# A convolution by two-step Fourier transforms on one Trainium2 core: real and imaginary rows contracted in one matmul, two column halves side by side

## The chip, the cores and the metric

The kernel runs on one core of one Trainium2 chip (trn2). The metric is the device time of one execution in microseconds, lower is better. A kernel is executed several times; the times and their median are given, and one further execution carries the hardware profiler. Engines are named as in the profile: PE is TensorE (PEld its weight loads), DVE VectorE, ACT ScalarE, POOL GpSimd, SP SyncE.

## The reference

Two branches read the same `x` (2048 rows, 640 columns, bfloat16); a gate per row mixes them.

```python
def reference(A_x, A_wqkv, A_wo, B_u, B_A_re, ..., B_Dskip, gate_w):
    # branch A: 32 heads of 20; each position attends to itself and 7 earlier
    # ones, 2 apart
    qkv = x @ wqkv
    logits = einsum("bhsd,bhswd->bhsw", q, kg) * scale     # 8 positions each
    o = einsum("bhsw,bhswd->bhsd", softmax(logits), vg)
    a = o @ wo
    # branch B: per column d a filter K of 2048 taps, then a long convolution
    P = exp(dt * A[:, :, None] * arange(L))                # D x 192 x L
    K = einsum("dn,dnl,dn->dl", C, P, dt * B).real
    y = irfft(rfft(pad(u)) * rfft(pad(K)))[:L] + u * Dskip
    g = sigmoid((x * gate_w).sum(-1, keepdims=True))
    return g * a + (1 - g) * y                              # u is x
```

## The kernel before

The program has two parts, each a list of tasks whose order over all engines is a table of numbers (`ORDER["main"]`, `ORDER["tail"]`): a row says which task comes next and, with a letter, on which engine an eviction runs (A for ACT, D for DVE). `Plan.emit` writes the instructions in that order, and each engine keeps its own part of it, first in, first out. `Plan.add` gives each task a duration, its dependencies (`deps`), order-only predecessors (`after`) and the buffers that it takes and gives back; the durations serve the search that made the table and reach no instruction.

"main" (to about 245 us) does the attention, the gate and the filter taps, and the first step of both Fourier transforms. `KGen` makes the taps: argument matmuls (L827), sines and exponentials on ACT (L842, L844), products on DVE (L864, L866), and small matmuls in four column groups of 32 (L882, into `kps`). The attention of 256 rows at a time is: products on DVE (L384), logits (L390), weighted values on DVE (`pv`, L453), their sums over heads in two column halves (L460, the "gathers"), and the output projection (L484) with its eviction (L493 or L495).

A transform of 4,096 points is split into 32 times 64. The **first step** is the 32-point one. Its data lie with partitions (4 column groups g, 32 times t1). One unit of it, made by `first` or `split` in `gated_mix_kernel`, yields 1,024 numbers in each of 128 partitions: the filter's first half of columns in ten units `f1`, its second half in ten units `fk` (five of them cut in two by `split`, which uses the `tb` buffers of the attention), the input's in twenty units `fu`. The data are the weights of the matmul, taken as every `st`-th column of `kc` (the filter) or `Usb` (the input), and a table of cosines and sines is streamed:

- `f1`, `fk` (L1329, halves L1352): four matmuls a unit, each with 128 columns of weights that lie 40 elements (80 bytes) apart and 256 streamed columns.
- `fu` (L1325): eight matmuls a unit, in two halves of the rows (64 partitions each, side by side), each with 128 columns of weights that lie 80 elements (160 bytes) apart and 128 streamed columns. The table is block diagonal, so each row half needs only its own half of it.

The result stands in a two-bank PSUM tile of the pool `ar`, of which there are two, and ACT or DVE evicts it (`evict`, L511 or L513) into `bufA` (filter, `Bk`) or `big` (input). In both, a partition is (c2, t2): c2 is one of two halves of the columns of x, t2 one of 64 times; and the free index f of 64 is (32 frequencies f1, real or imaginary).

"tail" (`fft_conv`) begins with the **second step**, for eight blocks `fb` of four frequencies f1. A unit (`trans`, L1095) makes the real (ro = 0) or imaginary (ro = 1) spectrum of two frequencies, of filter (k) or input (u): four matmuls of 128 by 128 weights and 320 streamed columns. The weights come from a table `phis` that holds the 64-point matrix twice on the diagonal, once for each c2, in the three forms real, imaginary and minus imaginary; for each frequency, a matmul on the real columns and one on the imaginary ones add up in PSUM. Each unit is evicted on ACT or DVE (`ev`) into `sp_k` or `sp_u`. Six DVE products and sums a block (`ta`, `tc`, L1123; `Y`, L1126) multiply the spectra. Then come the inverse steps (L1156, evictions into `bufA`; L1186) and the mix with the attention's result (L1192, L1195, L1200), and the stores (L1213).

The table `phis` takes eight loads of 4 frequencies: three from POOL in "main" (`load_phi`, tag `PHI`), three on SP at the start of the tail into tiles `PHX` (`more`), two more on SP into freed `PHI` tiles. The units of blocks 3 to 7 depend on their load (`ready`). SP also loads `psi` and the attention's result `gaF`, paced by the evictions (`paced`).

Of the kernel before, what the change touches and what calls it, by code (L numbers as in the profile page):

```python
# [13 lines left out]
F32 = mybir.dt.float32  # L14
# [26 lines left out]
def _attn_consts():  # L41
# [929 lines left out]
def _fft_consts():  # L971
# [6 lines left out]
    for g in range(4):  # L978
        f1b[g, :, g, :] = f1c.reshape(32, 64)
# [23 lines left out]
def fft_prefetch(ctx, tc, x, omS, keep):  # L1003
# [12 lines left out]
    def load_phi(k, eng=nc.gpsimd):  # L1016
        t = pre.tile([128, 4, 3, 128], BF16, name="PHI", tag="PHI", bufs=3)
        eng.dma_start(t[:], phi_d[:, 4 * k:4 * k + 4])
        return t
# [413 lines left out]
```

## Time and profile before

| | before |
|---|---|
| median of 3 runs | 314.68 us (314.07 to 315.07) |
| the profiled execution | 316.68 us |
| its span, first to last instruction | 314.9 us |
| PE, DVE, ACT busy | 286.3, 285.9, 285.2 us |
| mean granted TensorE clock | 0.978 |
| first step, `fu` units | 218.1 to 238.5 us |
| second step, first to last matmul | 244.75 to about 281.9 us |

In the profile's rows, `x` is a count; a row of the timeline gives start, duration (from the first start to the last end of a merged group), engine, line, operation, and out<-in. `128*64` beside a matmul is its weights' rows and columns, `128x320` what it streams. In the windows view each stretch has the busy time and the count of each engine, the granted clock, the share of the DMA engines and GB/s.

### The profile page before, as it was taken

The page shows a single profiled execution, that of the slowest core. Times are in us where ns is not written, and L with a number is a line of the kernel's source. Part 1 is how long each engine was busy: PE and PEld are TensorE (multiplying, and loading weights), DVE is VectorE, ACT ScalarE, POOL GpSimd, SP SyncE. Part 2 cuts the span into 40 slices and gives each one's busy share as a digit, 9 for nine tenths or more (in the row PEclk, how much of TensorE's full clock was granted, in tenths as well). Part 3 has the DMA queues.
Part 4 walks back from the last instruction along what each step waited for, and adds up shares of the span by engine and source line. Part 5 has one row for each costly group of instructions (what it writes and reads, how often), then busy time and mean ns, then how long its engine had stood idle before and what let it go on. Part 6 is the DMA issues. An engine that isn't in the chain of part 4 may idle for free. (4 is left out here: it accounts for less than half of the span.)

```text
span 314.9 us, 12073 instructions
## 1 busy us (share of the span) xinstructions
PE 286.3 (91%) x5268; PEld 169.8 (54%) x5268; DVE 285.9 (91%) x381; ACT 285.2 (91%) x431; POOL 56.9 (18%) x84
## 2 busy tenths in 40 slices
PE   8799999999999999999999989789999999979740
PEld 3455543444554554555555555447668676659730
DVE  4988999999999989999999999999888899998881
ACT  2789869999999999999999999999989799997890
POOL 8722440302000001111302022020120000000072
PEclk9799999999999999999999999999999999997995
DMA  7995679286111304537795694742493366591076
GB/s 260 363 237 140 183 200 168 81 176 149 24 36 21 106 8 122 108 89 214 192 264 126 127 212 94 153 103 79 169 334 115 131 214 167 113 167 20 4 174 161
DMA packets 47182, 45.70 MB, mean 145 GB/s; under 512 B 27034, under 2 KB 40650, under 8 KB 47130
## 3 DMA queue, kind: packets, MB, share of 16 engines
q1 hardware_dynamic: 40776, 26.68, 32.7%
q0 software_dynamic: 5392, 17.53, 21.7%
q8 instruction: 41, 0.67, 0.9%
q10 hardware_dynamic: 962, 0.73, 0.8%
q14 instruction: 11, 0.09, 0.1%
HBM read 29.60 MB, written 14.01 MB: 138 GB/s over the span
## 5 line engine op out<-in xcount | busy, mean ns | idle before, releaser
L319 PE MATMUL tb<-bufA 128*128 128x512 bf16 x300 | 76.4, 390 | 1.6 <-DMA bufA<-in_A_wqkv_dram 1.2
L842 ACT ACTIVATE big<-ar 128x740 bf16<-128x740 int16 (+1 forms) x72 | 57.6, 876 | 0.2
L827 PE MATMUL ar<-Rarg,L 64*128 64x212 bf16 (+4 forms) x600 | 47.8, 251 | 5.0 <-ACT big L842 2.2
L844 ACT ACTIVATE big<-ar 128x848 bf16<-128x848 f32 x60 | 49.8, 903 | 0.5 <-PE ar L827 0.2
L319 PEld LDWEIGHTS <-bufA 128*128 128x128 bf16 x300 | 31.8, 121 | 30.3 <-issue 9.9
L453 DVE TENSOR_TENSOR pv<-vc,asb 128x2048 bf16<-128x2048 bf16 x40 | 47.7, 1217 | 0.2 <-PE tb L460 0.2
L827 PEld LDWEIGHTS <-L 64*128 64x128 bf16 x600 | 20.7, 94 | 33.7 <-issue 30.8
L864 DVE TENSOR_TENSOR pt<-big 128x1024 bf16<-128x1024 bf16 x48 | 32.2, 702 | 1.5 <-PE kps L882 0.8
L882 PEld LDWEIGHTS <-pt 128*32 128x32 bf16 (+1 forms) x2560 | 23.1, 92 | 11.6 <-issue 9.4
L882 PE MATMUL kps<-qq,pt 128*32 128x21 bf16 (+1 forms) x2560 | 28.1, 174 | 0.6 <-ACT E L511 0.3
L484 PE MATMUL tb<-wo_sb,oT 128*128 128x320 bf16 x160 | 27.7, 301 | 0.9 <-ACT ga L493 0.7
L384 DVE TENSOR_TENSOR prod<-qA,kA 128x2048 bf16<-128x2048 bf16 x20 | 23.8, 1219 | 0.4 <-PE lg L390 0.3
L511 ACT ACTIVATE sp_u<-fp 128x640 bf16<-128x640 f32 x30 | 22.4, 876 | 1.7 <-PE fp L1095 1.7
L384 DVE TENSOR_TENSOR prod<-prj 128x2048 bf16<-128x2048 bf16 x20 | 23.8, 1218 | 0.0
L460 PE MATMUL tb<-pv,ind 128*64 128x512 bf16 (+1 forms) x192 | 22.3, 350 | 0.3 <-DVE pv L453 0.3
L511 ACT ACTIVATE sp_k<-fp 128x640 bf16<-128x640 f32 x30 | 22.2, 883 | 0.4 <-PE fp L1095 0.4
L866 DVE TENSOR_TENSOR qq<-big 128x1344 bf16<-128x1344 bf16 x24 | 21.2, 884 | 0.0
L1213 POOL DMA_DIRECT2D out_dram<-ot x14 | 7.8, 560 | 71.3 <-PE yp L1186 68.8
L1095 PEld LDWEIGHTS <-PHI 128*128 128x128 bf16 x160 | 15.6, 98 | 7.8 <-issue 1.8
L377 POOL DMA_DIRECT2D vc<-vS x16 | 11.5, 726 | 44.5 <-DVE pv L453 39.6
L484 PEld LDWEIGHTS <-oT 128*128 128x128 bf16 x160 | 13.5, 97 | 8.1 <-issue 3.6
L493 ACT ACTIVATE ga<-tb,g_sb 128x320 bf16<-128x320 f32 x28 | 15.2, 570 | 0.0
(171 smaller groups left out, 525.6 us busy)
## 6 DMA issues: line engine op xcount, KB each, us to landing
vc<-vS POOLq DMA_DIRECT2D x16, 327.5 KB, 5.4
gaS<-ga SPq DMA_DIRECT2D x8, 320.0 KB
Usb<-in_A_x_dram POOLq DMA_DIRECT2D x8, 320.0 KB, 5.0
gaF<-gaS SPq DMA_DIRECT2D x8, 320.0 KB
bufA<-in_A_wqkv_dram SPq DMA_DIRECT2D x3, 800.0 KB
L<-Sprm SPq DMA_DIRECT2D x76, 30.0 KB
asb<-aS SPq DMA_DIRECT2D x16, 128.0 KB
psi<-c_psi SPq DMA_DIRECT2D x4, 512.0 KB
```

The costliest lines, as they stand in the source:

```text
L319: nc.tensor.matmul(ppf, self.wq[:, which, kt, e::5], self.xT[:, c0 // 1024, kt, c0 % 1024:c0 % 1024 + SC], start=(kt == 0), stop=(kt == NK ...
L384: nc.vector.tensor_tensor(b[e][:], q[:, e, o:o + C].unsqueeze(1).to_broadcast([128, W, C]), win(k[:, e, :], o, W, DIL, C), ALU.mult)
L453: nc.vector.tensor_tensor(o, vw, b["asb"][:].unsqueeze(2).to_broadcast(sh), ALU.mult)
L460: nc.tensor.matmul(b["op", e][64 * a:64 * a + 64, 0:n, :], ind[:, 32:96], b["pv", e][:, w, a, 0:n, :], start=(w == 0), stop=(w == 3), skip ...
L484: nc.tensor.matmul(apf[:, :320], b["oT"][:, e, i * 128:(i + 1) * 128], wo_sb[:, e, hf * 320:(hf + 1) * 320], start=(e == 0), stop=(e == 4))
L511: nc.scalar.activation(o, i, ACT.Identity)
L827: nc.tensor.matmul(ar[:, g2, a0:a0 + ncol], L[rows, sb, gv, l0:l0 + 128], R[rows, c0:c0 + ncol], start=True, stop=True, tile_position=(64 ...
L842: nc.scalar.activation(d_[:, :, s0 * QW:s1 * QW], ar[:].bitcast(I16)[:, :, 0:2 * (s1 - s0) * QW:2], ACT.Sin, scale=SCL)
L844: nc.scalar.activation(dst[:, gp::2].rearrange("p g s n -> p g (s n)"), ar[:, :, 0:2 * EW], ACT.Exp)
L864: nc.vector.tensor_tensor(pt[:, :, k, :], gg[:, :, ::-1] if k else gg, e1, ALU.mult)
L866: nc.vector.tensor_tensor(qq[:], trg[:, :, KI:].rearrange("p a (v m) -> p a v m", v=2), exq[:, :, KI:].unsqueeze(2).to_broadcast([128, 32, ...
L882: nc.tensor.matmul(kps[32 * g:32 * g + 32, h, NM * ql:NM * ql + NM], pt[rows, k, v, :], qq[rows, k, v, :], start=(g not in started), stop= ...
```

## The change

The first step now puts real and imaginary parts into partitions: its tables are laid out as (real or imaginary, f1, g), a matmul takes only 64 columns of weights (t2, for one c2) and streams 128 columns, and the real part goes to PSUM partitions 0 to 63, the imaginary part to 64 to 127 (`tile_position=(0, 64 * r)`). All units, `fu` too, have one form: sixteen matmuls in eight such pairs, both of a pair with the same 64 weight columns. Those lie twice as far apart as before: 80 elements (160 bytes) in `kc`, 160 elements (320 bytes) in `Usb`. The odd and even units are now the two c2, so that the free index f of `bufA` and `big` is (f1, c2).

In the second step, real and imaginary rows are then contracted in one matmul of 128 rows: a unit has four matmuls, two frequencies times two c2; each has 64 columns of weights and 320 streamed columns, and the two c2 go to the two column halves. Nothing accumulates over two matmuls any more. The table has two forms of 64 columns for each frequency and is a third as large. Three loads from POOL, of 12, 12 and 8 frequencies, hold all of it, so the five loads in the tail and their waits are gone.

Both parts of `ORDER` are new numbers. Of the planned durations, `fu` goes from 0.25 to 0.47, `f1` and `fk` from 0.437 to 0.47, a half from 0.22 to 0.24, a unit of the second step from 0.566 to 0.28.

```diff
 ORDER = {"main": (
-    "0 14 40 -53 3 51 -5 -47 -1 49 -45 1D 45 1 9 1 -55 -3 4 13 43 1 -55 45 -46 54 -6 9D 4 1 -15 16 -46D 2 -17 47D 9 1 1 -57 "
...
+    "0 14 -13 3 6 -8 5D 43 1 -48 49 1 -47 2 46 1 7 1 1 1 -56 57 1D 4 1 -14 -2 -45 1 -7 68 -16 20 1 1D 4 1 -25 -37 -9 72D "
...
+    f1b = f1b.reshape(4, 32, 4, 32, 2).transpose(0, 1, 4, 3, 2)
     f1c = f1b.reshape(128, 256)
...
-    phis = np.zeros((64, 2, 32, 3, 2, 64), np.float32)
-    for c2 in range(2):
-        phis[:, c2, :, 0, c2, :] = Phi.real.transpose(1, 0, 2)
-        phis[:, c2, :, 1, c2, :] = Phi.imag.transpose(1, 0, 2)
-        phis[:, c2, :, 2, c2, :] = -Phi.imag.transpose(1, 0, 2)
-    phis = phis.reshape(128, 32, 3, 128)
+    pr, pi = Phi.real.transpose(1, 0, 2), Phi.imag.transpose(1, 0, 2)
+    phis = np.stack([np.stack([pr, pi], axis=2), np.stack([-pi, pr], axis=2)], axis=0).reshape(128, 32, 2, 64)
...
     def load_phi(k, eng=nc.gpsimd):
-        t = pre.tile([128, 4, 3, 128], BF16, name="PHI", tag="PHI", bufs=3)
-        eng.dma_start(t[:], phi_d[:, 4 * k:4 * k + 4])
+        n = min(12, 32 - 12 * k)
+        t = pre.tile([128, 12, 2, 64], BF16, name="PHI", tag="PHI", bufs=3)
+        eng.dma_start(t[:, 0:n], phi_d[:, 12 * k:12 * k + n])
...
-    early = []
-    for k in range(3, 6):
...
-        early.append(pl.add(f"tphi{k}", "S", 0.4, more, after=early[-1:], dma=1.6))
...
-                        for ri in range(2):
-                            kind = (0 if ri == 0 else 2) if ro == 0 else (1 if ri == 0 else 0)
-                            nc.tensor.matmul(fp[:, fl % 2, 0:320].rearrange("p (c x) -> p c x", x=32), phis[fb][:, fl, kind, :],
-                                             B[:, :, 2 * f1 + ri].rearrange("p c q g -> p c (q g)"), start=(ri == 0), stop=(ri == 1))
+                        for c2 in range(2):
+                            nc.tensor.matmul(fp[64 * c2:64 * c2 + 64, fl % 2, 0:320].rearrange("p (c x) -> p c x", x=32), phis[f1 // 12][:, f1 % 12, ro, :],
+                                             B[:, :, 2 * f1 + c2].rearrange("p c q g -> p c (q g)"), start=True, stop=True, skip_group_check=True, tile_position=(0, 64 * c2))
...
-                if name == "fu":
-                    by = b["by"] = b["bp"][:].rearrange("p a (b f) -> p (a b) f", f=64).rearrange("p (g q) f -> p g q f", g=4)
-                    for ql in range(4):
-                        for r in range(2):
-                            nc.tensor.matmul(by[:, 2 * r:2 * r + 2, ql], sf[64 * r:64 * r + 64, 4 * n + ql::st], P["F1c"][64 * r:64 * r + 64, 128 * r:128 * r + 128],
-                                             start=True, stop=True, skip_group_check=True, tile_position=(64 * r, 0))
-                    return
-                for ql in range(4):
-                    nc.tensor.matmul(b["bp"][:, ql, :], sf[:, 4 * n + ql::st], P["F1k"][:], start=True, stop=True)
+                st = sf.shape[1] // 64
+                b["bp"] = pa.tile([128, 8, 128], F32, name="bp", tag="ar")
+                F = P["F1c" if name == "fu" else "F1k"][:].rearrange("p (r x) -> p r x", r=2)
+                for q in range(8):
+                    for r in range(2):
+                        nc.tensor.matmul(b["bp"][64 * r:64 * r + 64, q, :], sf[:, 8 * (n // 2) + q + st // 2 * (n % 2)::st], F[:, r],
+                                         start=True, stop=True, skip_group_check=True, tile_position=(0, 64 * r))
...
+                evict(nc, en, d_[:, n // 2, n % 2::2], b["bp"][:].rearrange("p q (f g) -> p f q g", g=4))
```

What this makes of the order is shown at three places. The first is PE while the last chunk's attention ends, between its gathers (`tb` from `pv`) and the input's units (`bp` from `Usb`). Before, two units of eight matmuls stood together between gathers of eight:

```order
L460 LDWEIGHTS ind_82
L460 MATMUL tb_5694<-pv_102,ind_82 64x512
...
L1325 LDWEIGHTS Usb_3743
L1325 MATMUL bp_5705<-F1c_73,Usb_3743 128x2x64
...
L1325 MATMUL bp_5715<-F1c_73,Usb_3743 128x2x64
...
L460 MATMUL tb_5726<-pv_102,ind_82 64x512
```

In the changed kernel, a unit of sixteen matmuls stands after every four of a gather:

```order
L460 LDWEIGHTS ind_82
L460 MATMUL tb_5834<-pv_102,ind_82 64x512
...
L1308 LDWEIGHTS Usb_3790
L1308 MATMUL bp_5839<-F1c_73,Usb_3790 64x128
...
L460 MATMUL tb_5834<-pv_102,ind_82 64x512
...
L1308 MATMUL bp_5866<-F1c_73,Usb_3790 64x128
...
L460 MATMUL tb_5884<-pv_102,ind_82 64x512
```

A gather is now cut in two by a unit. After the last `kps` matmul of the taps, PE has twenty `fu`, one `f1` and ten `fk` units where it had eighteen, one and ten.

The second place is PE where the first step ends and the second begins (`fp` from `big` or `bufA` and the table `PHI`). Before, the filter's units came last and the input's spectrum first:

```order
L1352 MATMUL tb_5960<-F1k_74,kc_5889 128x256
L1095 LDWEIGHTS PHI_5919
L1095 MATMUL fp_5990<-big_605,PHI_5919 128x320
...
L1095 MATMUL fp_5995<-big_605,PHI_5919 128x320
...
L1095 MATMUL fp_6003<-bufA_78,PHI_5919 128x320
```

Now an input unit comes last and the filter's spectrum first:

```order
L1308 MATMUL bp_6351<-F1c_73,Usb_3790 64x128
L1079 LDWEIGHTS PHI_6055
L1079 MATMUL fp_6390<-bufA_78,PHI_6055 64x320
...
L1079 MATMUL fp_6395<-bufA_78,PHI_6055 64x320
...
L1079 MATMUL fp_6403<-big_599,PHI_6055 64x320
```

Three of the twenty input units moved in among the filter's at the end. The third place is SP's queue from the last store of the attention (`gaS`) to the first output. Before:

```order
L505 DMA gaS<-ga 128x2x640
L1074 DMA PHX_6008<-c_phi 128x1536
L1074 DMA PHX_6010<-c_phi 128x1536
L1074 DMA PHX_6117<-c_phi 128x1536
L1111 DMA psi<-c_psi 128x2048 x2
L1018 DMA PHI<-c_phi 128x1536 x2
L1111 DMA psi<-c_psi 128x2048 x2
L1114 DMA gaF<-gaS 32x16x320 x8
```

And now:

```order
L505 DMA gaS<-ga 128x2x640
L1095 DMA psi<-c_psi 128x2048 x4
L1098 DMA gaF<-gaS 32x16x320 x8
L1197 DMA out_dram<-ot_7301 32x2x320 x2
L1197 DMA out_dram<-ot_7280 32x2x320 x2
```

Five loads are gone from it, and nothing stands ahead of `psi` and `gaF` but their own pacing.

More of the change, by code (lines that the diff above doesn't have):

```diff
@@ L1068, in fft_conv @@
     ends, muls, turned, paces, last = [], {}, [], [], None
-    early = []
-    for k in range(3, 6):
-        def more(_, k=k):
-            t = sb.tile([128, 4, 3, 128], BF16, name=f"PHX{k}")
-            phis.append(t)
-            nc.sync.dma_start(t[:], phi_d[:, 4 * k:4 * k + 4])
-        early.append(pl.add(f"tphi{k}", "S", 0.4, more, after=early[-1:], dma=1.6))
     for fb in range(8):
         spec, sp = {}, {}
-        if 3 <= fb < 6:
-            ready = early[fb - 3]
-        elif fb >= 6:
-            ready = pl.add(f"tphi{fb}", "S", 0.4, lambda _, fb=fb: phis.append(P["load_phi"](fb, nc.sync)), deps=turned[8 * fb - 48:8 * fb - 40], after=[ready], dma=1.6)
-        else:
-            ready = None
         for n, (nm, ro) in enumerate((("k", 0), ("k", 1), ("u", 0), ("u", 1))):
@@ L1101, in ev @@
                     evict(nc, en, spec[nm, ro][:, :, 2 * h:2 * h + 2], spec[nm, ro, h][:, :, 0:320].rearrange("p f x -> p x f"))
-                m = pl.add(f"fp{fb}{nm}{ro}{h}", "P", 0.566, trans, deps=[ready], after=(turned[-8:-7] if fb else []) + (paces[fb - 2:fb - 1] if fb > 1 else []), acq=["fp" if h else "ar"])
+                m = pl.add(f"fp{fb}{nm}{ro}{h}", "P", 0.28, trans, after=(turned[-8:-7] if fb else []) + (paces[fb - 2:fb - 1] if fb > 1 else []), acq=["fp" if h else "ar"])
                 turned.append(m)
@@ L1115, in fft_conv @@
         if fb < 7:
-            paces.append(pl.add(f"paced{fb}", "S", (0.4, 0.4, 0.4, 0.8, 0.8, 0.8, 1.2)[fb], paced, deps=es, after=paces[-1:] or early, dma=(2.1, 2.1, 2.1, 3.4, 2.7, 2.7, 4.0)[fb]))
+            paces.append(pl.add(f"paced{fb}", "S", (0.4, 0.4, 0.4, 0.8, 0.8, 0.8, 1.2)[fb], paced, deps=es, after=paces[-1:], dma=(2.1, 2.1, 2.1, 3.4, 2.7, 2.7, 4.0)[fb]))
             paces[-1].waits = es
@@ L1318, in mm @@
                 sf = src()[:].rearrange("p a b -> p (a b)")
-                st = sf.shape[1] // 128
-                b["bp"] = pa.tile([128, 4, 256], F32, name="bp", tag="ar")
-                if name == "fu":
-                    by = b["by"] = b["bp"][:].rearrange("p a (b f) -> p (a b) f", f=64).rearrange("p (g q) f -> p g q f", g=4)
-                    for ql in range(4):
-                        for r in range(2):
-                            nc.tensor.matmul(by[:, 2 * r:2 * r + 2, ql], sf[64 * r:64 * r + 64, 4 * n + ql::st], P["F1c"][64 * r:64 * r + 64, 128 * r:128 * r + 128],
-                                             start=True, stop=True, skip_group_check=True, tile_position=(64 * r, 0))
-                    return
@@ L1331, in ev @@
             def ev(en):
-                if name == "fu":
-                    d_ = now["big"][:].rearrange("p (c f q g) -> p c f q g", c=NCH, f=64, q=8)
-                    evict(nc, en, d_[:, n // 2, :, 4 * (n % 2):4 * (n % 2) + 4, :], b["by"].rearrange("p g q f -> p f q g"))
-                    return
                 d_ = now["big"][:].rearrange("p (c f q g) -> p c f q g", c=NCH, f=64, q=8) if dst is None else dst
-                evict(nc, en, d_[:, n // 2, :, 4 * (n % 2):4 * (n % 2) + 4, :].rearrange("p f q g -> p f (q g)"),
-                      b["bp"][:].rearrange("p q (g f) -> p f (q g)", f=64))
@@ L1339, in first @@
-            m = pl.add(f"{name}{n}", "P", 0.25 if name == "fu" else 0.437, mm, deps=deps, after=after, acq=["ar"], eq=1024)
+                evict(nc, en, d_[:, n // 2, n % 2::2], b["bp"][:].rearrange("p q (f g) -> p f q g", g=4))
+            m = pl.add(f"{name}{n}", "P", 0.47, mm, deps=deps, after=after, acq=["ar"], eq=1024)
             if name == "f1":
@@ L1348, in mm @@
                 sf = half[1, "kc"][:].rearrange("p a b -> p (a b)")
-                st = sf.shape[1] // 128
-                b["bp"] = ps.tile([128, 2, 256], F32, name="tb", bufs=2)
-                for ql in range(2):
-                    nc.tensor.matmul(b["bp"][:, ql, :], sf[:, 4 * n + 2 * h + ql::st], P["F1k"][:], start=True, stop=True)
+                st = sf.shape[1] // 64
+                b["bp"] = ps.tile([128, 4, 128], F32, name="tb", bufs=2)
+                F = P["F1k"][:].rearrange("p (r x) -> p r x", r=2)
+                for q in range(4):
+                    for r in range(2):
+                        nc.tensor.matmul(b["bp"][64 * r:64 * r + 64, q, :], sf[:, 8 * (n // 2) + 4 * h + q + st // 2 * (n % 2)::st], F[:, r],
+                                         start=True, stop=True, skip_group_check=True, tile_position=(0, 64 * r))
             def ev(en):
-                evict(nc, en, Bk[:, HC + n // 2, :, 4 * (n % 2) + 2 * h:4 * (n % 2) + 2 * h + 2, :].rearrange("p f q g -> p f (q g)"),
-                      b["bp"][:].rearrange("p q (g f) -> p f (q g)", f=64))
-            m = pl.add(f"fk{n}h{h}", "P", 0.22, mm, deps=deps, after=after, acq=["tb"], eq=512)
+                evict(nc, en, Bk[:, HC + n // 2, n % 2::2, 4 * h:4 * h + 4], b["bp"][:].rearrange("p q (f g) -> p f q g", g=4))
+            m = pl.add(f"fk{n}h{h}", "P", 0.24, mm, deps=deps, after=after, acq=["tb"], eq=512)
             pl.add(f"fke{n}h{h}", "AD", {"A": 0.48, "D": 0.60}, ev, deps=[m], rel=[("tb", m)])
```

86 rows, old and new, of the table ORDER are left out of this document.

## The prediction

> **What bounds the kernel now.** I read the page's first part, then the busy times by stage, because an average hides which engine ends last where.
>
> ```profile
> PE 286.3 (91%) x5268; PEld 169.8 (54%) x5268; DVE 285.9 (91%) x381; ACT 285.2 (91%) x431; POOL 56.9 (18%) x84
> 160.00:219.60 59.60, 54.77 (x1391) 32.21 (x1388) 58.13 (x67) 59.27 (x91) 10.54 (x15) 1.00 0.60 144
> 219.60:244.75 25.15, 23.81 (x262) 17.51 (x257) 21.37 (x30) 23.18 (x36) 3.35 (x6) 1.00 0.59 205
> 244.75:283.76 39.01, 35.90 (x256) 24.88 (x255) 37.23 (x54) 36.18 (x60) 0.00 (x0) 1.00 0.61 154
> ```
>
> Each stretch's busy times are in the order PE, PEld, DVE, ACT, POOL. Three engines are equal on average, but the stages differ. Up to 219.6 ACT is the bound (59.27 of 59.60 us) and PE has 4.8 us free. From the last tap matmul at 219.6 to the second step at 244.75, where most of the first step is done, PE leads (23.81 of 25.15). In the second step DVE leads (37.23 of 39.01). The waits of the two bounded stages say the same; a row is the waiter, what it waited for, us, times, longest.
>
> ```profile
> DVE big L513 <- PE bp L1325: 2.8, 3, 1.0
> ACT big L511 <- PE bp L1325: 1.6, 4, 0.7
> ...
> ACT sp_u L511 <- PE fp L1095: 1.7, 2, 1.3
> ```
>
> From 219.6 on, the evictions of the input's units wait for PE. In the second step ACT waits for PE once for 1.3 us, at its start. So a cheaper second step gains at its start only, and a dearer first step costs in full from 219.6 on.
>
> **What a unit of the first step costs.** From the start of a group to the start of the next one on PE:
>
> ```profile
> 225.06 0.54 PE L1325 MATMUL bp<-F1c,Usb 64*128 64x128 bf16 x8
> 225.53 0.45 PE L484 MATMUL tb<-wo_sb,oT 128*128 128x320 bf16 x2
> ...
> 232.81 0.86 PE L1325 MATMUL bp<-F1c,Usb 64*128 64x128 bf16 x16
> 233.61 0.85 PE L484 MATMUL tb<-wo_sb,oT 128*128 128x320 bf16 x5
> 239.83 0.60 PE L1329 MATMUL bp<-F1k,kc 128*128 128x256 bf16 x4
> 240.27 0.86 PE L1352 MATMUL tb<-F1k,kc 128*128 128x256 bf16 x4
> ```
>
> One input unit takes 0.47 us, two take 0.80 (0.42 each on average); the second adds 0.33, so a pair of its matmuls takes 83 ns. A filter unit takes 0.44. The changed unit has eight pairs. No row here shows 64 strided columns loaded in a column half, so I bound a pair from both sides.
>
> From below, by column halves whose weights are not strided, the gathers, and the taps' small matmuls in four column groups:
>
> ```profile
> 210.35 0.62 PE L460 MATMUL tb<-pv,ind 128*64 128x512 bf16 x4
> 210.91 0.66 PE L1329 MATMUL bp<-F1k,kc 128*128 128x256 bf16 x4
> ...
> 226.37 1.05 PE L460 MATMUL tb<-pv,ind 128*64 128x512 bf16 x8
> 227.36 0.92 PE L1325 MATMUL bp<-F1c,Usb 64*128 64x128 bf16 x16
> ...
> 219.00 0.66 PE L882 MATMUL kps<-qq,pt 128*32 128x21 bf16 x64
> 219.58 0.58 PE L484 MATMUL tb<-wo_sb,oT 128*128 128x320 bf16 x3
> ```
>
> Four gather matmuls take 0.56, eight 0.99: two pairs more add 0.43, so a pair streams 512 columns in 0.215 and would stream 128 in 54 ns, if its loads hide. Eight pairs: 0.43. That loads of different column groups can run beside each other is seen in the taps: 64 matmuls, each with its own load of 32 columns, take 0.58, or 9 ns each. The 0.13 that four gather matmuls take beyond 0.43 is what changing the array's form costs.
>
> From above, by what stride does to a load. These rows give minimum/median/maximum in ns:
>
> ```profile
> L1095 PEld LDWEIGHTS <-PHI x160: 95/98/98, 243.8 to 281.4; 128*128 128x128 bf16 x160
> L1329 PEld LDWEIGHTS <-kc x60: 139/143/168, 169.2 to 243.5; 128*128 128x128 bf16 x60
> L1325 PEld LDWEIGHTS <-Usb x160: 154/180/198, 218.1 to 238.2; 64*128 64x128 bf16 x160
> ```
>
> 128 columns in a row take 98 ns, 80 bytes apart 143, 160 bytes apart 180. The input's pair would stream in 54 ns but takes 83: its strided loads, not its streaming, set it. If in the changed pair load and streaming came in turn, it would take 83 + 54 = 137 ns, a unit 1.10. I take 83 ns: a changed pair has to fetch as many strided weights (twice 64 columns by 128 rows) as the input's pair did (twice 128 columns by 64 rows). **Eight pairs: 0.66 us a unit.** It is nearest because it is the only row with strided weights in pairs.
>
> **The sum from 219.6 on.** Before: 18 input units at 0.42 and 11 filter units at 0.44, 12.4 us. Now 20 + 11 = 31 units at 0.66, 20.5: 8.1 more. The 1.3 us that PE is idle there take up part; I count 0.7. Gathers and units are now of one form, so five of the 0.13 us form changes go, 0.6. That leaves +6.8.
>
> **Up to 219.6.** Two input units have moved behind the boundary. Their evictions take 0.95 each on ACT:
>
> ```profile
> 222.95 4.73 ACT L511 ACTIVATE big<-bp 128x1024 bf16<-128x1024 f32 x5
> ```
>
> ACT is the bound there, but DVE is only 1.5 us behind, so I count half, -1.0. Nine `f1` units dearer by 0.22 put 2.0 us on PE, under its 4.8 us of idle time; as PE works in order, I count 0.5 for what they delay. Without that cover it would be 2.0. Together -0.5. The rest of the new order does the same work, and I count nothing for it, give or take 1.
>
> **The second step.** A unit falls from 0.55 to two pairs of 320 columns, 0.27 by the gathers' price (its table is not strided). What is late next:
>
> ```profile
> 257.26 0.71 PE L1095 MATMUL fp<-bufA,PHI 128*128 128x320 bf16 x4
> 257.81 0.71 PE L1095 MATMUL fp<-bufA,PHX 128*128 128x320 bf16 x4
> ...
> 244.75 1.25 PE L1095 MATMUL fp<-big,PHI 128*128 128x320 bf16 x8 [0.69 <-ACT bufA L511]
> 245.54 0.82 DVE L513 CAST sp_u<-fp 128x640 bf16<-128x640 f32 x1 [0.24 <-issue]
> 248.41 0.82 DVE L1123 TENSOR_TENSOR ta<-sp_u,sp_k 128x1280 bf16<-128x1280 bf16 x1
> 256.05 1.55 DVE L1123 TENSOR_TENSOR tc<-sp_u,sp_k 128x1280 bf16<-128x1280 bf16 x2
> 257.52 1.55 DVE L1126 TENSOR_TENSOR Y<-ta,tc 128x1280 bf16<-128x1280 bf16 x2
> ```
>
> The 64 units save 18 us of PE, but ACT needs 36.18 us for its 60 evictions and DVE 37.23 for its chain, in which two products take 1.47 us (256.05 to 257.52). Only the wait for the first product goes, 3.66 us from 244.75 to 248.41. Its four units need two evictions on each engine, twice 0.82, behind a first unit of 0.27 and the 0.3 us from a matmul's start to its end (0.71 less three spacings of 0.14): 2.2. That gains 1.4, and DVE's idle time of the whole stage caps the gain at 1.8. **I take -1.6.**
>
> The five loads of the table go from SP's queue (the first three took 1.29 us to issue, while PE and the evictions ran on). No wait of these two stages names a DMA, so they are worth nothing. Inverse steps and output are the same instructions: 0.
>
> ```profile
> 241.39 1.29 SPq L1074 DMA_DIRECT2D PHX<-c_phi  x3
> ```
>
> The profiled execution took 316.68 us (span 314.9 and 1.78 around it), 2.00 above the median of the runs, 314.68. 316.68 + 6.8 - 0.5 - 1.6 = 321.4, by the median **319.4 us**.
>
> **Rivals.**
>
> *The strided loads hide (faster).* Loads of 64 columns are half as long, the taps show that column groups load side by side, and a pair takes 54 ns. Then 31 units at 0.43 are 13.3 us, 0.9 more than before; less 0.6 for the form changes that is 0.3, and DVE and ACT, with two more evictions, become the bound of that stage: +1.0, against -1.0 ahead of it, and -1.6 in the second step: 313.1. It decides below the price at which the sum is zero: 31 c = 12.4 + 0.7 + 0.6 + 0.5 + 1.6, c = 0.51, or 64 ns a pair. Against it speaks the input's pair, whose two loads are side by side too (other rows) and still cost 83. Chance 0.34.
>
> *Load and streaming in turn (much slower).* At 1.10 a unit, 31 units are 34.1 us, 21.7 more, less 1.3: +20.4. Nine `f1` units dearer by 0.66 exceed PE's 4.8 us of idle time by 1.1, against -1.0; with -1.6 the time is 333.6. For it: the stride doubles, to 160 and 320 bytes. Against it: in the taps loads hide. Chance 0.20.
>
> A rule of the Trainium skill speaks for this rival: by "TensorEngine Tiling (Array Packing)", Restrictions, column tiling switches the fast weight load off, and by "TensorE: Matmul & The Clock Gate", LDWEIGHTS, a load then takes its columns divided by 1.2, 53 ns for 64. Two such loads in turn would make a pair 107 ns, a unit 0.85, and the sum, as an estimate, 325. The 9 ns of the taps' matmuls with 32 columns each speak against loads in turn; with stride no run shows it.
>
> *The second step does not run in pairs, or the new order is better or worse by more than 1 us elsewhere.* Without pairs a unit stays at 0.55, the -1.6 goes, and the time is 321.0. Against it: the gathers run in pairs. Chance 0.04.
>
> **Numbers.** A measurement of this kernel can tell about 0.3%, 0.9 us, from no change. The forecast, 0.42, has its own range of 316.8 to 321.7 (a pair between 72 and 92 ns, a unit between 0.58 and 0.74). Range for 8 in 10: 312.0, the first rival less 1, to 327.0, a pair of 107 ns and a little more; outside lie most of the second rival and the fringes of the first. Faster: 0.27 of the first rival and 0.02 of the rest, 0.29. The same: 0.10, 0.07 of it the first rival, where the order costs a little. Slower: 0.39 of the forecast, 0.20, 0.02: 0.61.
>
> **What would show it.** In the changed profile: the sixteen matmuls of an input unit, start to start, at 0.66 us (0.43 or 1.1 for the rivals); PE ahead of ACT and DVE from the last `kps` to the first `fp`, some 32 us apart instead of 25, with evictions waiting for `bp`; the first `ta` 2.2 us after the first `fp`, and DVE without a gap from there. Wrong: a unit below 0.51, a second step shorter by over 2 us, or a start of the last stage that is late before the first step is.

## The result, and the profile after

The changed kernel takes 342.99 us (median of 4 executions, 340.42 to 343.28), the kernel before beside it 314.88: a ratio of 1.087 [1.080, 1.094]. Forecast were 319.4 us. The profiled execution took 343.28 us (span 341.2).

The busy times by stage of the changed kernel, cut at the same events as before (end of the last `kps`, first `fp`, first inverse matmul); the columns are PE, PEld, DVE, ACT, POOL, the granted clock, the DMA share and GB/s:

```profile
160.00:229.20 69.20, 64.45 (x1564) 41.43 (x1547) 59.92 (x70) 60.50 (x89) 10.04 (x14) 0.93 0.57 127
229.20:271.80 42.60, 42.51 (x575) 38.31 (x574) 24.36 (x38) 24.64 (x31) 3.84 (x7) 0.89 0.30 104
271.80:309.97 38.17, 24.60 (x262) 16.01 (x260) 36.51 (x52) 36.93 (x61) 0.00 (x0) 0.99 0.53 123
309.97:341.20 31.23, 17.04 (x576) 15.33 (x576) 21.22 (x35) 20.78 (x34) 7.75 (x14) 0.83 0.35 89
```

The stage up to the last `kps` ends 9.6 us later (229.2 against 219.6), the stretch from there to the second step takes 42.6 us instead of 25.15, the second step 0.8 less, the rest the same. In the long stretch PE is busy for all but 0.1 us, and ACT and DVE, with 24 us of work each (23 and 21 in the kernel before), wait. Who waits there, for what, and for how long in all:

```profile
ACT big L511 <- PE bp L1308: 7.9, 13, 1.4
DVE bufA L513 <- PE tb L1329: 6.7, 6, 1.2
...
ACT bufA L511 <- PE bp L1308: 4.3, 4, 1.5
```

The units themselves, on the timeline of PE (start, duration, then the group):

```profile
241.43 1.00 PE L1308 MATMUL bp<-F1c,Usb 128*64 128x128 bf16 x16
242.26 0.60 PE L460 MATMUL tb<-pv,ind 128*64 128x512 bf16 x4
...
265.03 1.49 PE L1308 MATMUL bp<-F1k,kc 128*64 128x128 bf16 x16
266.31 0.84 PE L1329 MATMUL tb<-F1k,kc 128*64 128x128 bf16 x8
```

From start to start an input unit takes 0.83 us (eight pairs of 104 ns), a filter unit 1.28 (pairs of 160 ns). Forecast were 0.66 for both. The weight loads alone, as the changed kernel's line 1308 has them (minimum, median, maximum in ns):

```profile
L1308 PEld LDWEIGHTS <-Usb x320: 184/205/243, 231.6 to 271.6; 128*64 128x64 bf16 x160
...
L1308 PEld LDWEIGHTS <-kc x240: 232/272/277, 172.2 to 269.9; 128*64 128x64 bf16 x120
```

By these records 64 columns that lie 160 bytes apart take longer to load than 128 columns did before (143 at 80 bytes, 180 at 160). The records of neighbouring loads overlap: a whole pair takes 160 ns. The first product of the second step comes on DVE 2.81 us after the first `fp` (271.80); forecast were 2.2:

```profile
274.61 0.83 DVE L1107 TENSOR_TENSOR ta<-sp_u,sp_k 128x1280 bf16<-128x1280 bf16 x1 [0.18 <-ACT sp_u L511]
```

### The profile page after: what moved, and what is told of

It reads as the page before. It is cut to its first block, busy times and chain, and to the rows that moved or that the text cites. A ratio compares the mean times of both kernels' runs of the same rounds, so it can differ in the third digit from the quotient of the medians.

```text
span 341.2 us, 12873 instructions
## 1 busy us (share of the span) xinstructions
PE 302.1 (89%) x5668; PEld 190.4 (56%) x5668; DVE 289.8 (85%) x391; ACT 286.6 (84%) x421; POOL 58.1 (17%) x86
## 5 line engine op out<-in xcount | busy, mean ns | idle before, releaser
L319 PE MATMUL tb<-bufA 128*128 128x512 bf16 x300 | 75.0, 384 | 1.6 <-ACT prj L511 0.6
L842 ACT ACTIVATE big<-ar 128x740 bf16<-128x740 int16 (+1 forms) x72 | 56.1, 845 | 1.6 <-PE ar L827 1.3
L827 PE MATMUL ar<-Rarg,L 64*128 64x212 bf16 (+4 forms) x600 | 48.8, 254 | 6.3 <-ACT big L842 4.0
L882 PE MATMUL kps<-qq,pt 128*32 128x21 bf16 (+1 forms) x2560 | 29.2, 175 | 0.3 <-ACT E L511 0.2
L1079 PEld LDWEIGHTS <-PHI 128*64 128x64 bf16 x256 | 16.0, 109 | 19.5 <-issue 18.6
L460 PE MATMUL tb<-pv,ind 128*64 128x512 bf16 (+1 forms) x192 | 24.1, 362 | 0.0
L511 ACT ACTIVATE big<-bp 128x1024 bf16<-128x1024 f32 x16 | 16.3, 1024 | 8.6 <-PE bp L1308 8.3
L1308 PE MATMUL bp<-F1k,kc 128*64 128x128 bf16 x240 | 22.1, 336 | 0.6 <-ACT bufA L842 0.3
L1308 PEld LDWEIGHTS <-kc 128*64 128x64 bf16 x240 | 20.9, 269 | 1.4 <-issue 1.1
L1308 PEld LDWEIGHTS <-Usb 128*64 128x64 bf16 x320 | 20.0, 206 | 2.5 <-issue 2.0
```

The source lines that it names most:

```text
L319: nc.tensor.matmul(ppf, self.wq[:, which, kt, e::5], self.xT[:, c0 // 1024, kt, c0 % 1024:c0 % 1024 + SC], start=(kt == 0), stop=(kt == NK ...
L460: nc.tensor.matmul(b["op", e][64 * a:64 * a + 64, 0:n, :], ind[:, 32:96], b["pv", e][:, w, a, 0:n, :], start=(w == 0), stop=(w == 3), skip ...
L511: nc.scalar.activation(o, i, ACT.Identity)
L827: nc.tensor.matmul(ar[:, g2, a0:a0 + ncol], L[rows, sb, gv, l0:l0 + 128], R[rows, c0:c0 + ncol], start=True, stop=True, tile_position=(64 ...
L842: nc.scalar.activation(d_[:, :, s0 * QW:s1 * QW], ar[:].bitcast(I16)[:, :, 0:2 * (s1 - s0) * QW:2], ACT.Sin, scale=SCL)
L882: nc.tensor.matmul(kps[32 * g:32 * g + 32, h, NM * ql:NM * ql + NM], pt[rows, k, v, :], qq[rows, k, v, :], start=(g not in started), stop= ...
```

## Experiments

Theory 1 after the result: a load of weight columns that are not adjacent has a price for each column, set by how far apart they lie; in column halves the 64 columns of a load are fetched one after the other, and this, not streaming, sets the unit. Theory 2: the new order is bad. Theory 3: load and streaming come in turn, whatever the distance. A fourth came up on the way.

### The price of a load by itself (e4, e8)

A program that does nothing but groups of matmuls, each group of one form and one distance. Its core, for pairs in column halves (`s` is the distance in elements of 2 bytes):

```python
for r in range(2):
    nc.tensor.matmul(t[64 * r:64 * r + 64, 0, c:c + 128], W[:, o:o + 63 * s + 1:s], S[:, 128 * r:128 * r + 128],
                     start=True, stop=True, tile_position=(0, 64 * r))
```

> A program of its own that leaves the whole computation out (it stores x) and runs 24 groups of matmuls for each form and stride of the weights: pairs of 64 columns in column halves with 128 streamed columns (c64) at 43 strides, pairs of 128 columns in row halves (r128), 128 by 128 weights with 256 streamed (f128), 64 columns in one half only (one64), pairs with 32 streamed columns (n64), 32 columns in four column groups (c32). Theory 1: c64 about 54 ns a pair at stride 1 (streaming sets it), 160 at 80 elements, 104 at 160 elements; n64 the same as c64 at 80 and 160, because the fetch alone sets it; r128 about 83 at 80 elements; f128 about 110 (256 streamed) up to 40 elements. Theory 3: c64 at stride 1 is 100 ns or more, and n64 shorter than c64 by the streaming of 96 columns, 40 ns.

The groups of this first run have no names of their own in the trace; by the counts of its windows a pair takes 56 ns adjacent and up to 4 bytes apart, 60 at 8, and 113 to 135 at most distances from 16 to 512 bytes; 160 at 160 and 162 bytes, from where it falls to 125 at 180, and 148 at 256. The second run has the forms that matter under names; the end of a name is the distance in bytes in Roman numerals (B viii = 8, B clx = 160, B cccxx = 320).

> A program of its own that leaves the whole computation out (it stores x): 32 groups of matmuls for each of 23 forms and strides, each with a name. By the first such program: pairs of 64 columns in column halves 56 ns adjacent, 60 at 8 bytes, 121 at 16 and 80, 160 at 160 (also from another start, if the stride alone decides), 125 at 180, 117 at 320 (104 from another start, if the place decides, as in the kernel); one load alone 160 at 160 bytes; short pairs (32 streamed columns) 160; four loads of 32 columns 80 at 160 bytes, 62 at 180, 58 at 320; row halves 62 adjacent, 81 at 160 bytes, 67 at 192; full loads with 256 streamed 110 throughout.

On its timeline the time from the start of a group to the start of the next, divided by 32, is the price of a pair (or of one load, or of four):

```profile
27.05 1.98 PE L31 MATMUL pairAdjacent<-S,W 128*64 128x128 bf16 x64
28.86 2.17 PE L31 MATMUL pairBviii<-S,W 128*64 128x128 bf16 x64
30.86 4.02 PE L31 MATMUL pairBxvi<-S,W 128*64 128x128 bf16 x64
34.70 4.01 PE L31 MATMUL pairBlxxx<-S,W 128*64 128x128 bf16 x64
38.53 5.30 PE L31 MATMUL pairBclx<-S,W 128*64 128x128 bf16 x64
43.65 5.30 PE L31 MATMUL pairBclxOff<-S,W 128*64 128x128 bf16 x64
48.77 4.23 PE L31 MATMUL pairBclxxx<-S,W 128*64 128x128 bf16 x64
52.83 4.01 PE L31 MATMUL pairBcccxx<-S,W 128*64 128x128 bf16 x64
56.66 3.83 PE L31 MATMUL pairBcccxxOff<-S,W 128*64 128x128 bf16 x64
60.32 3.69 PE L31 MATMUL pairBcccxxOfg<-S,W 128*64 128x128 bf16 x64
63.84 5.29 PE L38 MATMUL oneBclx<-S,W 128*64 128x128 bf16 x32
68.97 3.54 PE L38 MATMUL oneBcccxx<-S,W 128*64 128x128 bf16 x30
...
81.09 3.13 PE L42 MATMUL quadBclx<-S,W 128*32 128x128 bf16 x128
84.05 0.70 PE L42 MATMUL quadBclxxx<-S,W 128*32 128x128 bf16 x31
...
92.93 2.76 PE L46 MATMUL rowsBclx<-S,W 64*128 64x128 bf16 x64
95.50 2.18 PE L46 MATMUL rowsBcxcii<-S,W 64*128 64x128 bf16 x64
97.61 3.67 PE L49 MATMUL fullAdjacent<-S,W 128*128 128x256 bf16 x32
101.11 3.66 PE L49 MATMUL fullBlxxx<-S,W 128*128 128x256 bf16 x32
104.61 3.68 PE L49 MATMUL fullBclx<-S,W 128*128 128x256 bf16 x32
```

A pair takes 57 ns adjacent ((28.86 - 27.05) / 32), 63 at 8 bytes, 120 at 16 and at 80, 160 at 160 bytes from either start, 127 at 180, and 120, 114 or 110 at 320 bytes, by the start. One load alone at 160 bytes takes 160 ns as well (68.97 - 63.84): the two of a pair run side by side. Four loads of 32 columns take 92 at 160 bytes on average (84.05 - 81.09), but this group ran in part at a lower clock: 0.50 at its start, 0.71 over 81.1 to 84.0. Where the clock is back at 1.00, four loads take 80 ns (52 matmuls from 82.94 to 83.98), half of a pair's 160. Row halves, the form of the input's units before, take 80 at 160 bytes and 66 at 192; full loads with 256 streamed columns take 109 adjacent and at 80 bytes, and the group at 160 bytes is as long, so their streaming covers them.

Theory 1 holds for the filter's 160 ns, which e8 gives as well. For the input it gives 110 to 120 where the kernel has 104; the start matters, and how is left open. Theory 3 falls: adjacent pairs take 57 ns. One thing is not separated: a load of 128 columns at 160 bytes hides behind 109 ns of streaming, where 64 columns in a half take 160. Whether that is only the number of columns fetched one after the other, or also a slower kind of load in column halves, no run here shows. The rule that the prediction cited from the Trainium skill ("TensorE: Matmul & The Clock Gate", LDWEIGHTS: columns divided by 1.2, 53 ns for 64) does not contradict the adjacent pair's 57 ns, if the two loads run side by side, but streaming alone would give 54; it says nothing of distance, and here the measurement decides.

### Adjacent columns in the changed kernel (e1)

```diff
-    ... sf[:, 8 * (n // 2) + q + st // 2 * (n % 2)::st], F[:, r],
+    j = 8 * (n // 2) + q + st // 2 * (n % 2)
+    ... sf[:, 64 * j:64 * j + 64], F[:, r],
```

> The changed kernel, but the first step takes 64 adjacent columns of the data as weights instead of every 80th (filter) or 160th (input); this changes which numbers go into which transform, all else is as in the changed kernel. Theory 1 (each strided column that a weight load fetches has a price set by the stride; 160 ns a pair at 160 bytes, 104 at 320): a unit falls from 1.28 and 0.83 us to between 0.43 and 0.55, the stretch from the last kps to the first fp from 43 us to 24 to 28, the time to 311 to 320 us, and the granted clock there returns to about 1. Theory 2 (the searched order is bad): the time stays at 338 to 345 us. Theory 3 (load and streaming come in turn for loads in a column half, whatever the stride): a unit of 0.85 or more, 325 to 343 us.

319.56 us, 1.012 [1.005, 1.019] of the kernel before: 23.4 us less than the changed kernel, with the same instructions in the same order. Stages, and two units on PE, of this run:

```profile
160.00:221.50 61.50, 55.90 (x1580) 33.63 (x1566) 59.41 (x69) 59.26 (x89) 10.02 (x14) 0.97 0.64 145
221.50:248.60 27.10, 25.90 (x574) 20.07 (x573) 23.55 (x38) 24.15 (x32) 3.83 (x7) 1.00 0.47 163
```

```profile
231.06 0.64 PE L1309 MATMUL bp<-F1c,Usb 128*64 128x128 bf16 x16
231.50 0.63 PE L460 MATMUL tb<-pv,ind 128*64 128x512 bf16 x4
...
241.67 0.64 PE L1309 MATMUL bp<-F1k,kc 128*64 128x128 bf16 x16
242.12 0.42 PE L1331 MATMUL tb<-F1k,kc 128*64 128x128 bf16 x8
```

Both kinds of units take 0.44 us. The stretch falls from 42.6 to 27.1, the last `kps` comes 7.7 us earlier, and the granted clock in the stretch is back at 1.00 from 0.89. The low clock did not make the filter's pairs slow: they take the same 160 ns in the kernel, where the clock is 0.50 from 266 to 268, and in e8, where it is 1.00. The input's units, 0.83 at full clock, took 0.97 and 1.00 in that stretch of the changed kernel (from 262.78 and from 270.80). Theory 1 carries 23.4 of 28.1 us. The time is at the upper end of its range, so 5 us have another cause.

### Half of it at a time (e10, e11)

The filter's columns 72 elements apart (e10), or the input's alone adjacent (e11):

```diff
-    ... sf[:, j::st], F[:, r],
+    ... sf[:, j::st] if name == "fu" else sf[:, j::72][:, 0:64], F[:, r],          (e10)
+    ... sf[:, 64 * j:64 * j + 64] if name == "fu" else sf[:, j::st], F[:, r],      (e11)
```

> The changed kernel, with the filter's 64 columns taken 72 elements (144 bytes) apart instead of 80 (160 bytes), so other numbers go into the filter's transform; number of loads and matmuls as in the changed kernel. Theory 1 (the price of a column depends on the very distance, 119 ns a pair at 144 bytes, 160 at 160): a filter unit 0.95 to 1.0 us instead of 1.28, twenty units 0.3 less each, the last kps 3 us earlier and the stretch behind it 3 us shorter, the time 336 to 338 us. Rival (any wide distance has one price): 343, as the changed kernel.

> The changed kernel, with adjacent columns for the input's units alone; other numbers go into the input's transform. Theory 1, as a sum of prices: twenty units fall from 0.83 to 0.96 to about 0.5, 8 us less, all of it behind the last kps; the time 334 to 336 us, the filter's units still 1.28 and the last kps still near 228.5. Rival (the two kinds of units hide each other's price, so that only both together pay): 340 us or more.

e10 takes 335.5 us (1.065 [1.060, 1.069]), 7.5 less than the changed kernel, 0.5 below the range given; e11 334.24 (1.061 [1.057, 1.065]), 8.75 less. In e10 a filter unit takes 0.96:

```profile
261.31 1.13 PE L1309 MATMUL bp<-F1k,kc 128*64 128x128 bf16 x16
262.27 0.65 PE L1330 MATMUL tb<-F1k,kc 128*64 128x128 bf16 x8
```

Moving the filter's columns 16 bytes closer together, with no matmul more or less, gives 7.5 us. The prices add: e11 gains what its twenty units lose, and its last `kps` stays at 228.4.

### Four column groups of 32 (e6, and once more e7)

```diff
-    for r in range(2):
-        nc.tensor.matmul(b["bp"][64 * r:64 * r + 64, q, :], sf[:, j::st], F[:, r], ..., tile_position=(0, 64 * r))
+    for k in range(2):
+        for r in range(2):
+            p = 64 * r + 32 * k
+            nc.tensor.matmul(b["bp"][p:p + 32, q, :], sf[:, j + 32 * k * st:j + 32 * k * st + 31 * st + 1:st], F[:, r], ..., tile_position=(0, p))
```

> The changed kernel, with each matmul of a column half cut into two of 32 weight columns in column groups of their own; the same numbers are computed. Theory 1 with loads of different column groups fetched side by side (in the strided program one load alone takes 160 ns and two in both halves also 160): four loads of 32 columns take half of it, 80 ns at 160 bytes and 52 to 60 at 320, a filter unit 0.64 to 0.75 us, an input unit 0.43 to 0.50, from the last kps to the first fp 28 to 32 us, the time 319 to 326 us. Rival (the fetches of all groups go through one place, one column after the other): units stay at 1.28 and 0.83 or more, 343 us or more. Rival (each load instruction has a price of its own of 40 ns or more): a unit of 32 loads 1.28 or more, 343 us or more.

> The run e6 once more with a profile only, as a second look at its units: the same durations within 2%.

(The second label speaks of the old order; that kernel does not have it.) 335.55 us, 1.066 [1.060, 1.071]; e7 332.28. The units came near what was expected for the filter (0.64 to 0.75), half of 1.28 and a little, and less well for the input (0.43 to 0.50):

```profile
227.78 0.87 PE L1311 MATMUL bp<-F1k,kc 128*32 128x128 bf16 x32
228.57 0.41 PE L460 MATMUL tb<-pv,ind 128*64 128x256 bf16 x3
...
238.61 0.75 PE L1311 MATMUL bp<-F1c,Usb 128*32 128x128 bf16 x32
239.29 0.62 PE L460 MATMUL tb<-pv,ind 128*64 128x512 bf16 x4
```

0.79 and 0.68. So loads of different column groups are fetched side by side, as theory 1 has it, and the rival of one place for all fetches falls. The time was missed by over 9 us. Part of it is that PE stands still with no wait named, five times ahead of its units, 5.3 us in all and up to 2.3; 3.1 us of it lie between the last `kps` and the second step, where 1,075 matmuls are started instead of 575. What stops PE there is not shown. PE's wait:

```profile
PE bp L1311 <- issue: 5.3, 5, 2.3
```

e7 is the same program, and its units agree with those of e6, but its last `kps` comes 4.6 us earlier (222.7 against 227.3). So far can two executions of one program differ ahead of that point; a difference of a few us there, between single executions, does not by itself show the effect of an edit.

### The order (e2, e3, e5)

Only the table of the first part is exchanged: the new one in the kernel before (e2), the old one in the changed kernel (e3), the old one with adjacent columns (e5, which is e1 with it).

```diff
-ORDER = {"main": (the changed kernel's numbers), "tail": ...
+ORDER = {"main": (the numbers of the kernel before), "tail": ...
```

> The kernel before with the changed kernel's order of the first part (the table of numbers of main); first step and second step are as before. Theory 1 (strided fetches): 312 to 319 us, since nothing of the array's work differs from before. Theory 2 (the order): 335 us or more.

> The changed kernel with the order of the first part that the kernel before has; matmuls and second step are as changed. Theory 1 (strided fetches): 337 to 350 us, about as the changed kernel or slower. Theory 2 (the order): 320 us or less.

> The run e1 (64 adjacent columns as weights; which numbers go into which transform is changed) with the order of the first part that the kernel before has. Theory 1 (strided fetches, and beside them an order that costs 4 to 5 us, as the run of the old code in the new order has it, 319.7 against 314.8): the last kps and the first fp come as before (219 and 244 to 246 us), the rest takes 68.8 us as in e1 against 70.2 before, together 312 to 316 us. If the order costs nothing with cheap loads: 319.6, as e1.

e2 takes 319.7 us (1.012 [1.004, 1.021]) where the kernel before has 314.8; e3 340.34 (1.079 [1.071, 1.087]); e5 322.66 (1.021 [1.014, 1.029]). Theory 2 is not the main cause, as e3 shows. With the old matmuls the new order costs 4.9 us. With the changed ones the medians differ by 2.6, but the executions overlap (339.62 to 341.8 with the old order, 340.42 to 343.28 with the new). With adjacent columns it is the old order that takes longer, by 3.1 us of the medians (e5 against e1), and the fastest executions are alike (318.59 and 318.86). So these runs show no price of the order by itself: what it costs depends on the matmuls that it is used with. I had expected up to 319 of e2 and 312 to 316 of e5; both were missed. Where e2 loses it, in the busy times of the stages well ahead of the change, first the kernel before, then e2:

```profile
100.00:160.00 60.00, 59.13 (x1398) 31.54 (x1383) 56.90 (x81) 59.49 (x90) 7.44 (x10) 1.00 0.46 120
160.00:217.00 57.00, 52.17 (x1269) 30.09 (x1266) 56.11 (x65) 56.79 (x88) 10.54 (x15) 1.00 0.63 150
```

```profile
100.00:160.00 60.00, 57.20 (x1394) 31.60 (x1407) 58.14 (x82) 58.21 (x89) 8.94 (x13) 1.00 0.42 111
160.00:217.00 57.00, 50.38 (x1261) 29.67 (x1258) 53.98 (x63) 55.16 (x84) 10.18 (x15) 1.00 0.68 153
```

ACT, the bound there, is idle for 0.7 us of these 117 in the kernel before and for 3.6 in e2. Most of it is in gaps that no wait of the trace names, so which rows of the table cost it is left open.

### The second step alone (e9)

First step and order of the first part from the kernel before, second step, table and second order from the changed one.

> The first step and the order of the first part from the kernel before, the second step, its table and the order of the second part from the changed kernel; the second step then contracts rows that were laid out for the old one, so the numbers are not the reference's. Theory 1: the second step's own gain stands without the first step's price: from the first fp to the end 68.5 to 69 us instead of 70.2 (37.4 us for the second step, as the two runs with adjacent columns had it, instead of 39.0), the time 312.5 to 314 against 314.6. Rival (the gain seen there came from evictions that had moved into the first part): 314.5 or more.

315.45 us against 314.25, 1.003 [1.000, 1.006]: no gain. Its last two stages, and one microsecond near the start of the inverse steps (PEclk is the third number from the end):

```profile
245.24:283.00 37.76, 24.41 (x258) 16.10 (x260) 36.60 (x52) 36.01 (x60) 0.00 (x0) 1.00 0.55 125
283.00:314.20 31.20, 17.11 (x576) 15.32 (x576) 21.25 (x35) 20.93 (x34) 7.73 (x14) 0.78 0.35 88
```

```profile
285.00:286.00 1.00, 1.00 (x24) 1.00 (x22) 0.78 (x1) 0.60 (x1) 0.00 (x0) 0.50 0.00 0
```

The second step is 1.3 us shorter (37.7 from the first `fp` at 245.24 to the first inverse matmul at 282.94, before 39.01), as forecast. But 0.6 us of that is lost just ahead of it. The new order of the second part begins with the filter's spectrum, and in the old first step the filter's units are evicted last: the first `fp` now waits 1.30 us, until DVE is done with `bufA` (at 245.1) and the small cast behind it, where it waited 0.69 before:

```profile
245.24 0.73 PE L1078 MATMUL fp<-bufA,PHI 128*64 128x320 bf16 x8 [1.30 <-DVE om L1056]
```

And the inverse steps begin with PE at half clock. That made a fourth theory: PE now pauses longer there (2.39 us instead of 1.93), and the clock falls.

### The input at 144 bytes in the kernel before (e12)

```diff
-    ... sf[64 * r:64 * r + 64, 4 * n + ql::st], ...
+    ... sf[64 * r:64 * r + 64, 4 * n + ql::72][:, 0:128], ...
```

> The kernel before, with the input's 128 columns taken 144 bytes apart instead of 160; other numbers go into the input's transform. Theory 1 (160 bytes are a dear distance: a pair in row halves 81 ns there, 62 at 144 in the strided program): the input's second unit in a row adds 0.25 to 0.27 us instead of 0.33, eighteen units behind the last kps 1 to 1.5 us less, the time 313 to 314 against 314.6. Rival (streaming sets the pair): 314.6.

314.13 us against 314.25, 1.000 [0.996, 1.004]: no change that can be measured, where 1 to 1.5 us were expected. Its stretch behind the last `kps`, and its last stage:

```profile
218.60:243.42 24.82, 22.87 (x258) 16.96 (x258) 21.37 (x30) 23.16 (x36) 3.34 (x6) 1.00 0.59 206
...
282.43:311.90 29.47, 15.84 (x576) 13.89 (x576) 21.05 (x35) 20.42 (x34) 7.73 (x14) 0.88 0.38 94
```

PE does 0.9 us less in the stretch (22.87 against 23.81), which becomes 0.3 us shorter: ACT's 23.16 us are then above PE's. The last row shows something else: here the clock stays at 1.00 at the start of the inverse steps, and the last stage takes 29.5 us, in the profile of the kernel before 31.14. In that profile the clock falls there.

### Filling the pause (e13, e14, e15)

Six matmuls ahead of the first inverse one, into a PSUM tile that it starts anew; in e9 (e13), in the kernel before (e14), in e5 (e15).

```diff
+    for k in range(6):
+        nc.tensor.matmul(q["cp", cb][:, 0].rearrange("p l x -> p (l x)"), GAB[:, 0, :], bufA[:, 0:512], start=True, stop=True)
```

> The run e9 (old first step, new second step), with six matmuls of 128 by 128 weights and 512 streamed columns added on PE ahead of the first inverse matmul, into a PSUM tile that the first real matmul starts anew. In e9's profile PE is idle for 2.39 us there and then runs at a granted clock of 0.5 for about 3.4 us, and the inverse steps and output take 31.2 us; in the kernel before's run with 144 bytes the clock stayed at 1.00 there and they took 29.5. Theory 4 (the new second step's 1.3 us are given back because PE's longer pause lets the clock fall at the inverse steps): the clock stays at 1.00, the last stage takes 29.5 to 30 us, the time 313.5 to 314.3 instead of 315.45. Rival (the clock falls whatever PE does in the pause, or costs nothing): 315 to 316.

> The kernel before with the same six matmuls in its pause of 1.93 us ahead of the inverse steps. Theory 4: those of its executions that showed a mean clock of 0.974 to 0.980 and 315.4 us or more become like the others, 313.7 to 314.9; the median 313.8 to 314.3, and the spread narrower. Rival: as before, 314.3, with the spread of before, or 1 us slower if the matmuls delay the first inverse matmul.

> The run e5 (adjacent columns, old order) with the same six matmuls. Theory 4: its last stage falls from 33.0 us to 29.5 to 30.5, the time from 322.66 to 318.5 to 320, near e5's fastest execution (318.59, the one with a mean clock of 0.983 where the others had 0.964). Rival: 322 or more.

e13 takes 315.97 us (ratio 1.002 [0.998, 1.006]), e14 315.59 (1.002 [0.999, 1.005]), e15 320.05 (1.013 [1.008, 1.019]); the kernel before took 315.03 beside them. In all three profiles the clock stays at 1.00 over the pause and behind it, but the fill waits for an eviction and then holds up the first inverse matmul: in e13 it comes 3.0 us after the last `fp` (1.65 of waiting, 1.38 of fill) and not 2.39:

```profile
283.20 1.46 PE L1139 MATMUL cp<-bufA,GAB 128*128 128x512 bf16 x5 [1.65 <-ACT sp_u L511]
284.58 2.42 PE L1142 MATMUL cp<-GAB,Y 64*128 64x128 bf16 x80
```

e15 took 2.6 us less than e5, but that is not all the fill: in the profiles, whose spans are 5.7 us apart, the first inverse matmul already comes 3.6 us earlier (285.80, behind the fill, against 289.42), and only 2.1 us are gained after it. e13 and e14 did not fall.

The clocks of the single executions fit theory 4 better than the times do. Of the 19 executions of the kernel before beside e9, 13 have a mean clock of 0.985 or more and take 313.7 to 314.9 us; the other six, at 0.974 to 0.980, take 315.4 to 318.2. All ten of e9 are at 0.974 to 0.984. With the fill, five of twelve are back at 0.985 or more, at 314.3 to 315.0. Against it: e12 and e10 kept their clock over unfilled pauses of 1.93 and 2.39 us, and e14 has 0.985 or more in ten of twelve executions and is no faster. So why the clock falls is not shown, and e9's missing gain is explained only in part: 0.6 us go to the wait ahead of its second step, and none of its executions has the mean clock that most of the kernel before have.

## Why the prediction was wrong

The sign and the place were right: PE became the bound of the first step, and evictions waited for `bp`. Two sizes were wrong, one assumption failed, and a small gain was given back. Starts in the profiled executions (of the last group of `kps`, of the first `fp` and of the first inverse matmul), and their spans, in us:

| run | last `kps` | first `fp` | first inverse | span |
|---|---|---|---|---|
| before | 219.0 | 244.75 | 283.76 | 314.9 |
| after | 228.6 | 271.80 | 309.97 | 341.2 |
| e1 adjacent | 220.9 | 248.60 | 286.30 | 317.4 |
| e6 four groups | 227.3 | 265.15 | 303.16 | 333.9 |
| e10 filter at 144 bytes | 225.6 | 265.29 | 303.31 | 333.7 |
| e11 input adjacent | 228.4 | 263.35 | 301.39 | 332.6 |
| e2 old code, new order | 223.0 | 250.87 | 289.88 | 320.2 |
| e3 new code, old order | 226.0 | 268.06 | 307.01 | 338.6 |
| e5 adjacent, old order | 220.4 | 250.60 | 289.42 | 321.2 |
| e9 second step alone | 218.9 | 245.24 | 282.94 | 314.2 |

**The price of a pair: the step that failed.** "I take 83 ns: a changed pair has to fetch as many strided weights" counted weights. What counts is how many columns stand one behind the other in a column group, and how far apart they lie. Pairs cost 160 ns in the filter and 104 in the input at full clock, a unit 1.28 and 0.83 (0.94 and more behind other forms and at half clock). 11 x 1.28 + 20 x 0.94 = 33 us from the last `kps` on, with 0.94 as the mean of the input's units on the timeline; forecast were 20.5. Most of these 12.4 us is what the stretch came out longer than said (17.45 more than before instead of 6.8, so 10.7; PE's idle time gave 1.25 instead of 0.7, and the other matmuls there became shorter by more than was counted). The price of the filter's units had no term of its own, although their distance is half the input's; and the upper bound, 137 ns, was too low, because it was built from the input's pair as well.

**Up to the last `kps`: also wrong.** The dearer `f1` units were to lie under PE's 4.8 us of idle time, 0.5 us being counted. Nine of them at 1.28 instead of the 0.44 to 0.5 of adjacent columns cost 7.0 to 7.6, and e1's last `kps` is 7.7 us earlier than that of the changed kernel. So about all of it showed, and PE is idle for 4.8 us of the longer stage as before (69.20 less 64.45). My reading, which no run tests: that idle time is spread over waits, the longest of 0.9 us in the kernel before, and covers no block of 1.3 us.

**The new order: "I count nothing for it, give or take 1".** It costs 4.9 us with the old matmuls (e2). With the changed ones it is 2.6 by the medians of executions that overlap (e3), and with adjacent columns the old order is the slower one (e5).

**The second step: right by itself, not seen in the time.** -1.6 was taken; it is -0.8 in the changed kernel and -1.3 in e1 and e9. The first product came 2.21 us after the first `fp` in e9, as worked out (2.2), and 2.81 in the changed kernel, where the last first-step units are still being evicted. Yet e9's time does not fall: 0.6 us is lost to the wait ahead of its first `fp`, and what takes back the rest was only argued, above.

**The rivals.** Load and streaming in turn came nearest in time (333.6), but is not what happens: short pairs with 32 streamed columns take about 160 ns at 160 bytes in the programs of strided loads, as long as with 128, so streaming hides behind the fetch. If the strided loads had hidden, the time would have been 319.6 (e1), and not 313.1. The old order does not mend that (322.66, e5), so it is not the order alone. Part is the last stage, 31.1 us in e1, which begins at half clock, against 29.5 in e12; the rest is left open.

**The sum.** Against 321.4 for this execution 343.28 were measured, 21.9 more: 10.1 up to the last `kps` (9.6 and not -0.5), 10.7 in the stretch, 0.8 in the second step, 0.1 in the rest, and 0.3 around the span (2.08 instead of 1.78), less rounding.

No run was faster than the kernel before by more than the measurement can tell.

## What to carry to other kernels

Price a weight load by the columns that are fetched one after the other in a column group and by the bytes between them, and measure that in a strip of matmuls before a layout is built on it: here 64 columns in a column half, 160 bytes apart, cost 160 ns, four loads of 32 columns 80, and loads of all 128 columns hid behind 109 ns of streaming. Don't count the idle time of an in-order engine as cover before you have looked at its single gaps. An order of many engines' work that was searched with one set of durations is itself a part of the change, and has to be timed with the old code too; what it costs there need not be what it costs with the new code.

## What the runs showed of the hardware

- A pair in column halves with 128 streamed columns takes 57 to 63 ns where its weight columns are adjacent or up to 8 bytes apart; from 16 bytes on 110 to 135 ns at most distances, and 160 at 160 bytes. Four loads of 32 columns take 80 at 160 bytes. In row halves 160 bytes cost 80 ns and 192 bytes 66. A distance of 144 or 180 bytes (119, 127 ns) is cheaper than 160.
- The filter's pair takes as long at half the granted clock as at full, 160 ns.
- PE can be busy for the whole of a window by its records and have its granted clock at 0.50. The changed kernel while the filter's second half is transformed (what lowers the clock is not shown: in e8 the same pairs of 160 ns ran for 10 us at 1.00):

```profile
266.00:268.00 2.00, 2.00 (x30) 2.00 (x30) 0.69 (x1) 1.02 (x1) 0.00 (x0) 0.50 0.00 0
```

- A pause of PE of 1.9 to 2.4 us is, in some executions, followed by 3 us or more at half clock, and in others by none: the last stage took 31.1 us with it and 29.5 without, in the kernel before and e12.
- In e6, with about a thousand small matmuls in 37 us, PE stopped for up to 2.3 us with no wait named; the cause is not shown.
